# Polysketch attention, then a top-1 routed expert layer, on one core: a new hand-written order, fewer POOL rests behind the row scatters, and the zeroing of the row buffer in pieces

## The chip, the cores and the metric

The kernel runs on one core of a Trainium2 chip. The engines of the core run side by side, each through its own queue in order, and wait for one another on semaphores: TensorE (PE; its weight loads are listed as PEld), VectorE (DVE), ScalarE (ACT), GpSimd (POOL) and SyncE (SP, which here issues the loads). The metric is the device time of one execution in microseconds; lower is better. Before the change the median of five runs is 212.13 us (211.49 to 216.92).

## The reference

Four sequences of 1088 tokens with four heads of 32 numbers go through an attention without softmax. Each key and query is projected with two 8x32 matrices S1 and S2, and the outer product of the two projections (64 numbers, phi) takes its place. The result goes token by token through one of eight experts.

```
a = x @ S1.T;  b = x @ S2.T                        # x is q or k, per head
phi(x)[i*8 + j] = a[i] * b[j]
kv = sum over s of phi(k)[s] (x) v[s];   z = sum over s of phi(k)[s]
attn[s] = (phi(q)[s] @ kv) / (phi(q)[s] @ z + 1e-06)
x = attn as 4352 rows of 128 (four heads side by side)
logits = x @ w_gate;  e = argmax(logits);  gate = softmax(logits)[e]
out = gate * (relu(x @ w1[e]) @ w2[e])             # w1: 128x1024, w2: 1024x128, each of 8
```

## The kernel before

**Attention.** A batch b (0 to 3) is done in two chunks c of 512 tokens; the 64 tokens left of each batch go in pairs of batches r. Names in the order are made of these: k00 is the keys of batch 0, chunk 0; kr0 the left-over keys of batches 0 and 1; q and qr likewise. A chunk's steps (`features`, lines 347 to 399) are .t (PE turns four 128x128 blocks), .x (ACT copies them to SBUF), .a (PE projects, eight matmuls), .l (ACT copies the low part of the sums), .s (DVE adds it) and .o (DVE, L395, the outer product of 1024 numbers a partition). Keys then have .v (L404 and L408, PE: 40 small matmuls that add to kv), and a batch ends with e{b}: .r adds the left-over keys, .k copies (ACT), .t multiplies with the heads and the gate weights (PE), .c (ACT) and .m and .z (DVE) write the matrix kvx. Queries are turned in two halves (.T and .U on PE, .c and .d the copies on ACT), multiplied with kvx (.n and .N, PE, L522 or L526), and then divided: .p (ACT), .e (DVE reciprocal), .g (DVE, gate logits, L546) and .y (DVE, the 128 numbers of the row, L552), each with a 2 behind it for the second half.

**Routing.** r{b} finds the expert of each token of batch b: .a and .b (DVE: maximum and one-hot, L606), .x (ACT) and .c (DVE) the gate weight, .p (PE, L620 and L622) counts the tokens before each, .d (DVE, L635) makes the row number. Then r{b}.s{u} are eight or nine scatters on POOL (L641): each sends 128 rows of 130 words (128 numbers, gate weight, token number) to their place in the DRAM buffer xs_dram, where each expert has its own stretch of 4352 rows. The first 128 rows of each stretch are filled beforehand, with zeros and a token number that names no token, by one DMA on SP (L981) from the tile fill.

**Experts.** Tiles j of 128 rows are read back from xs_dram and go through one expert each. Tiles 0 to 9 need batches 0 and 1 in xs_dram, 10 to 17 batch 2 too, and from 18 on all four. A tile's steps (`expert_tile`, lines 816 to 922): .l (SP, L824, load of xg), .x (PE turns it, L846), .c (ACT copy), .w (DVE copies w1 of the expert, L858), .u and .U (PE, L863, two banks of eight matmuls), .r and .q (Relu; .q on DVE from tile 10 on), .d (PE, L898, sixteen matmuls with w2, into the bank py; its address in w2 is read from a table by each engine that needs it, L811), .y (ACT scales by the gate weight) and .s (POOL, L912, scatter to the output). 34 tiles always run. Up to seven more stand in three optional parts of 4, 2 and 1 tiles (`part`, line 1007), each under a branch (L1010). With this data the part of four is skipped and the other two run; it stands behind the .U of tile 25 and ahead of the .d of tile 24. t0, t1 and t2 (DVE) count which tile belongs to which expert.

**What sets the order.** The program is put out step by step as the list ORDER (line 20) has it; each engine's queue gets its part of that. After the last name of ORDER a loop (line 1037) puts out the rest. Buffers are taken from rings in the order of the program: a step that takes one of the eight PSUM banks waits for the step that last read it. Behind a scatter POOL does a number of small MEMSETs on one row of fill (`breathe`, line 563): three behind those of batches 0, 2 and 3, one behind those of batch 1 (`RESTS`), and two behind the output stores of tiles 0 to 11. On SP the first loads are put out at once, then the fill, then k, v and q of batch 3 as their buffers come free, then the left-over rows of batches 2 and 3 (k_rem, v_rem, q_rem), then the weights of the experts.

Of the kernel before, what the change touches and what calls it, by code (L numbers as in the profile page):

```python
# [17 lines left out]


ORDER = """  # L20
S.t k00.t k00.x S.m k01.t k01.x k00.a kr0.t k00.l kr0.x k00.s k00.o k01.a k01.l kr0.a k01.s k01.o q00.t q00.x
kr0.l q01.t k00.v q00.a k10.t q01.x q01.a k01.v kr0.s kr0.o q00.l q00.s e0.r k11.t k10.x q00.o q01.l q01.s
k10.a q01.o e0.k e0.t e0.m q00.U k11.x k11.a e0.z k10.l k10.s k10.o e0.c q00.d q01.U k11.l q01.T k11.s k11.o
q00.N q00.T q01.d q01.N q01.c q00.p2 q00.e2 q00.y2 q00.c q01.p2 q00.g2 q01.e2 q01.y2 q01.g2 q01.n q01.p q01.e
q01.g q01.y q00.n q00.p qr0.t q11.t q21.t qr0.x qr0.a q20.t q11.x q11.a q20.x q00.e q00.g r0.a r0.x r0.b r0.c
k31.t qr0.l qr0.s q00.y r0.p r0.d r0.s7 r0.s2 r0.s1 r0.s5 r0.s0 r0.s6 r0.s3 r0.s4 k10.v k11.v e1.r k31.x qr0.o
q21.x q21.a q11.l q11.s kr1.t qr0.T e1.k q10.t q21.l q20.a q10.x e1.t q11.o q21.s q20.l q21.o e1.c q11.U e1.m
e1.z q10.a qr0.c q11.d q11.T kr1.x q20.s q20.o q10.l q10.s k30.t q11.c k30.x qr0.n qr0.p k20.t q10.o qr0.e
qr0.y qr0.g q11.N kr1.a q11.p2 q11.e2 kr1.l kr1.s k20.x q11.y2 q11.n q11.p q10.U q10.d k30.a k30.l q11.g2
q10.T q11.e q10.c q11.y k30.s q20.T q10.N k30.o q10.p2 q10.e2 q11.g q10.g2 q10.y2 k21.t k21.x q10.n q10.p  # L30
k20.a q31.t q20.c q10.e q10.g r1.a r1.b q31.x k31.a q21.T r1.x k31.l kr1.o r1.c q30.t q30.x k31.s k21.a q10.y
# [9 lines left out]
j2.s j1.s t1.d j5.l j3.U j3.q j4.u j5.x j5.c j4.U j4.q j7.l j6.x j6.c j4.r r3.p q30.y j9.l j8.l r3.c j7.x j5.w
j5.u j7.c j5.r j5.U j5.q r3.d r3.s2 r3.s6 j3.d r3.s1 j6.w j6.u j4.d j6.r j3.y j7.w j6.U j11.l j0.y j0.s j8.x
j8.c j9.x j9.c j6.q j7.u j10.l j8.w j4.y r3.s4 j9.w j7.U j12.l j10.w j5.d t2.a t2.b t2.c t2.d j7.q j5.y j7.r
j8.u j8.U j11.w j11.x j9.u j9.U r3.s8 j12.w j5.s j9.q j6.d j6.y j13.l j10.x j10.c j12.x j12.c j7.d j8.q j10.u
j10.U j15.l j11.c j13.w r3.s5 r3.s3 j11.u j10.q j8.r j8.d j12.u j12.U j9.r j9.d j8.y j12.r j10.r j11.U j11.q
# [13 lines left out]


@with_exitstack
def kernel(
# [155 lines left out]
    for b in range(B):  # L218
        t = new(f"x_rows{b}", [128, J + 1, XW])
        x_rows.append(t)  # L220
        lgh.append(lgh[b - 2] if b > 1 else new(f"lgh{b}", [128, J + 1, H * E]))
# [125 lines left out]
    def features(x, n, srcs, take_dst, keeps):  # L347
        st = {}

        @op(x + ".t")  # L350
        def _():
            t = st["tp"] = banks.take()
            for i, s in enumerate(srcs()):
                nc.tensor.transpose(t[:, ts(i, 128)], in_=s, identity=ident)  # L354
# [35 lines left out]
        def _():  # L390
            s = st["s"]
# [3 lines left out]
            nc.vector.tensor_tensor(dst, a[:, :, :, None].broadcast_to([128, n * 4, R, R]),  # L395
                                    b[:, :, None, :].broadcast_to([128, n * 4, R, R]), ALU.mult)
# [419 lines left out]
    def expert_tile(j):  # L816
# [75 lines left out]
        @op(x + ".d")  # L892
        def _():
            r = word(tiles[j][0], [PE], (E - 1) * F)
            t = s["py"] = banks.take()
            for c in range(8):
                h = s["hTa"] if c < 4 else s["hTb"]
                nc.tensor.matmul(t[:, :DM], lhsT=h[:, ts(c % 4, 128)], rhs=w2_all[:, ds(r + c * DM, DM)],  # L898
# [181 lines left out]
```

## Time and profile before

| what | value |
|---|---|
| median of five runs | 212.13 us |
| the profiled execution | 211.94 us, of which the span from the first to the last instruction is 210.1 us |
| granted clock of TensorE in it | 0.999 |
| PE busy | 199.6 us (95%), 2107 matmuls |
| PEld busy | 195.2 us (93%) |
| DVE busy | 120.1 us (57%) |
| ACT busy | 80.2 us (38%) |
| POOL busy | 106.9 us (51%), 108 of its instructions the MEMSETs of 240 ns |
| DMA | 23.32 MB, 111 GB/s over the span |

The shares are means over stages that differ: until about 69 us attention and routing run, with many short steps that pass from engine to engine, and behind it the expert tiles. So a stage's table and the timeline tell more than the shares. A line of the timeline gives the start, the duration, the engine, the line of the kernel, the operation with its operands, a count of like instructions in a row, and in brackets the idle time of the engine before it with what ended that. "issue" is time in which the engine waited for nothing that the profile shows. A "q" behind an engine's name is its sequencer (branches, semaphores, register loads).

### The profile page before, as it was taken

What the parts mean: (1) busy time and instruction counts of PE and PEld (TensorE: products, weight loads), DVE (VectorE), ACT (ScalarE), POOL (GpSimd) and SP (SyncE); (2) the same over time, 40 slices, a digit from 0 to 9 for tenths busy, and PEclk for the clock granted to TensorE, in tenths of its full rate; (3) what the DMA queues carried; (4) which work ended last, traced back from release to release, by engine and by line L of the source; (5) the groups of instructions that cost most, each with busy time, mean ns of one, the idle gap of its engine ahead of it and who ended that gap; (6) DMA issues with size and microseconds to landing.
All of it is one profiled execution on the core that took longest, in us unless ns stands there. A gap on an engine that the chain in (4) does not pass through costs nothing. (4 is left out here: it accounts for less than half of the span.)

```text
span 210.1 us, 6120 instructions
## 1 busy us (share of the span) xinstructions
PE 199.6 (95%) x2107; PEld 195.2 (93%) x2107; DVE 120.1 (57%) x381; ACT 80.2 (38%) x218; POOL 106.9 (51%) x211
## 2 busy tenths in 40 slices
PE   7999979999798999999999999999998999999991
PEld 7799869998697999999999999999997999999991
DVE  4598896889988887998105324346245433251410
ACT  2456437563443635342332243332332333223220
POOL 6100047767940477868767776878521264046043
PEclk9999999999999999999999999999999999999999
DMA  4999989999712200021011102123310120001000
GB/s 148 295 317 276 257 225 268 370 377 382 272 45 75 63 28 25 30 76 51 28 51 43 39 29 75 50 66 102 95 46 16 36 60 15 0 16 36 17 24 16
DMA packets 29279, 23.32 MB, mean 111 GB/s; under 512 B 5866, under 2 KB 27116, under 8 KB 29248
## 3 DMA queue, kind: packets, MB, share of 16 engines
q1 hardware_dynamic: 26304, 18.15, 30.6%
q0 software_dynamic: 2400, 4.50, 6.4%
q8 instruction: 19, 0.31, 0.6%
q10 hardware_dynamic: 544, 0.26, 0.4%
q14 instruction: 12, 0.10, 0.2%
HBM read 17.81 MB, written 5.55 MB: 111 GB/s over the span
## 5 line engine op out<-in xcount | busy, mean ns | idle before, releaser
L863 PE MATMUL bank<-xgT,wide 128*128 128x128 f32 x592 | 72.3, 275 | 0.0
L863 PEld LDWEIGHTS bank<-xgT,wide 128*128 128x128 f32 x592 | 69.3, 192 | 0.0
L641 POOL DMA_INDIRECT xs_dram<-x_rows,row_i x34 | 35.9, 1056 | 46.1 <-DVE row_i L635 22.6
L889 DVE TENSOR_SCALAR hTb<-bank 128x512 f32<-128x512 f32 x27 | 18.6, 692 | 64.5 <-PE bank L863 44.6
L912 POOL DMA_INDIRECT out_dram<-y,to x23 | 22.7, 988 | 38.8 <-ACT xgT L851 20.2
L898 PE MATMUL bank<-w_all,hTa 128*128 x296 | 39.3, 276 | 0.9 <-DVEq L1010 0.9
L898 PE MATMUL bank<-w_all,hTb 128*128 x296 | 39.2, 275 | 0.0
L898 PEld LDWEIGHTS bank<-w_all,hTa 128*128 128x128 f32 x296 | 36.0, 192 | 1.2 <-issue 1.1
L898 PEld LDWEIGHTS bank<-w_all,hTb 128*128 128x128 f32 x296 | 36.0, 192 | 0.0
L907 ACT ACTIVATE y<-bank,xg 128x128 f32<-128x128 f32 x37 | 13.1, 368 | 54.4 <-PE bank L898 54.4
L880 ACT ACTIVATE hTa<-bank 128x512 f32<-128x512 f32 x37 | 21.9, 600 | 22.8 <-PE bank L863 19.7
L858 DVE COPY wide<-w_all 128x1024 f32 x39 | 27.6, 725 | 2.5 <-issue 2.3
L566 POOL MEMSET fill<- 1x130 f32 x108 | 26.0, 240 | 3.6
L912 POOL DMA_INDIRECT out_dram<-y,xg x18 | 18.5, 1029 | 9.3 <-issue 6.4
L395 DVE TENSOR_TENSOR wide<-sum 128x1024 f32<-128x1024 f32 (+1 forms) x18 | 20.4, 1139 | 0.6
L366 PE MATMUL bank<-s_cat,xT 128*128 128x128 f32 x136 | 19.0, 280 | 0.0
L366 PEld LDWEIGHTS bank<-s_cat,xT 128*128 128x128 f32 x136 | 16.7, 192 | 0.4 <-ACT xT L359 0.2
L522 PE MATMUL bank<-kvx,q_pT 128*128 128x82 f32 x128 | 15.4, 272 | 0.0
L522 PEld LDWEIGHTS bank<-kvx,q_pT 128*128 128x128 f32 x128 | 15.0, 192 | 0.0
L359 ACT COPY xT<-bank 128x512 f32<-128x512 f32 (+1 forms) x20 | 10.3, 526 | 9.6 <-PE bank L354 9.5
L851 ACT COPY xgT<-bank 128x128 f32<-128x128 f32 x41 | 10.0, 265 | 7.7 <-PE bank L846 7.5
L510 ACT COPY q_pT<-bank 128x512 f32<-128x512 f32 (+1 forms) x18 | 9.8, 567 | 1.5 <-PE bank L502 1.3
(156 smaller groups left out, 179.1 us busy)
## 6 DMA issues: line engine op xcount, KB each, us to landing
w_all<-in_moe_w_dram SPq DMA_DIRECT2D x16, 512.0 KB, 7.5
xg<-xs_dram SPq DMA_DIRECT2D x41, 65.0 KB, 1.8
wide<-in_v_dram SPq DMA_DIRECT2D x4, 512.0 KB, 5.6
wide<-in_q_dram SPq DMA_DIRECT2D x4, 512.0 KB
wide<-in_k_dram SPq DMA_DIRECT2D x3, 512.0 KB, 11.2
xs_dram<-fill SPq DMA_DIRECT2D x1, 585.0 KB
xs_dram<-x_rows,row_i POOLq DMA_INDIRECT x34
out_dram<-y,to POOLq DMA_INDIRECT x23
```

The lines of the kernel that those rows point to most:

```text
L366: nc.tensor.matmul(t[:, ts(i, 128)], lhsT=st["xT"][:, ts(i, 128)], rhs=s_cat.rearrange("p w t g r -> p (w t g r)"), start=True, stop=True)
L395: nc.vector.tensor_tensor(dst, a[:, :, :, None].broadcast_to([128, n * 4, R, R]), b[:, :, None, :].broadcast_to([128, n * 4, R, R]), ALU.mult)
L522: nc.tensor.matmul(o, lhsT=lhsT, rhs=kvx[b][:, hp].rearrange("p g c -> p (g c)"), start=True, stop=True)
L566: nc.gpsimd.memset(fill[0:1], 0.0)
L641: d = nc.gpsimd.indirect_dma_start(out=xs_dram[:], out_offset=bass.IndirectOffsetOnAxis(ap=st["row"][:, u:u + 1], axis=0), in_=x_rows[b][: ...
L858: nc.vector.tensor_copy(out=s["w1"], in_=w1_all[:, ds(r, F)])
L863: nc.tensor.matmul(t[:, ts(c, 128)], lhsT=s["w1"][:, ts(c0 + c, 128)], rhs=s["xT"], start=True, stop=True)
L880: nc.scalar.activation(s["hTa"], s["ha"], AF.Relu)
L889: nc.vector.tensor_scalar(s["hTb"], s["hb"], 0.0, None, ALU.max)
L898: nc.tensor.matmul(t[:, :DM], lhsT=h[:, ts(c % 4, 128)], rhs=w2_all[:, ds(r + c * DM, DM)], start=(c == 0), stop=(c == 7))
L907: nc.scalar.activation(s["y"], s["py"][:, :DM], AF.Copy, bias=0.0, scale=s["xg"][:, DM:DM + 1])
L912: d = nc.gpsimd.indirect_dma_start(out=out[:], out_offset=bass.IndirectOffsetOnAxis(ap=s["to"](), axis=0), in_=s["y"], in_offset=None, bou ...
```

## The change

- ORDER is another list of the same steps, carried a little further (up to j14.d as before, but with the first steps of tiles 16, 18 and 19 among them), with one drain of POOL in it.
- RESTS: no MEMSET behind the scatters of batch 0, two behind every other one of batch 1 (the second, fourth and so on), two behind those of batches 2 and 3.
- The bank py of tile 24 is taken ahead of the optional part of four tiles and not behind it.
- xs_dram is filled by two DMAs from x_rows3 (the rows of batch 3, zeroed by DVE at the start and given the token number that names none by POOL): eight rows of 520 bytes lie side by side in one run of 4160. They are put out behind the load of k of batch 3, no longer ahead of it. The true token numbers of x_rows3 are written by POOL after k11.o.
- The copies k00.x and k01.x are halved between DVE and ACT, and late_constants are put out after k01.x and no longer after S.m. S.m follows S.t at once.

```diff
 ORDER = """
...
-q01.g q01.y q00.n q00.p qr0.t q11.t q21.t qr0.x qr0.a q20.t q11.x q11.a q20.x q00.e q00.g r0.a r0.x r0.b r0.c
-k31.t qr0.l qr0.s q00.y r0.p r0.d r0.s7 r0.s2 r0.s1 r0.s5 r0.s0 r0.s6 r0.s3 r0.s4 k10.v k11.v e1.r k31.x qr0.o
-q21.x q21.a q11.l q11.s kr1.t qr0.T e1.k q10.t q21.l q20.a q10.x e1.t q11.o q21.s q20.l q21.o e1.c q11.U e1.m
...
-r1.p q21.c r1.d r1.s6 r1.s2 k20.l k20.s r1.s3 q31.a q20.U qr1.t r1.s8 qr1.x k21.l r1.s0 q20.d k30.v k20.o
-q30.a k20.v r1.s1 k21.s k21.o k21.v q31.l k31.o r1.s5 e2.r e2.k qr1.a q31.s q30.l e2.t q31.o e2.m e2.z t0.a
-q30.s q30.o k31.v t0.b t0.c e2.c e3.r q21.U e3.k e3.t e3.m q31.U q21.d q20.n q31.d qr1.l q21.n q21.p qr1.s
...
-qr1.T q31.p2 q31.e2 q31.g2 q31.y2 q30.p r2.x qr1.c q31.n q31.p q31.e q31.y r1.s7 q31.g q30.e2 q30.g2 r2.p j0.l
-j0.x j0.c r2.d j2.w r2.c r2.s5 qr1.n qr1.p j1.l j1.x j0.u j2.l j1.c j0.U j3.l j0.r r2.s2 t0.d j0.q j2.x j2.c
...
+q10.l q11.U q01.c q00.p2 q11.d q01.N q01.p2 q10.s q10.o q01.n q00.e2 q00.y2 q01.e2 q01.g2 q01.y2 qr0.t q00.g2
+q01.p qr0.x k10.v k11.v e1.r q01.e q01.g qr0.a e1.k qr0.l kr1.t kr1.x r0.a r0.b q10.U q10.d k20.t k20.x qr0.s
+qr0.o q10.T e1.t e1.m e1.z kr1.a e1.c r0.x q01.y q11.T r0.c r0.p r0.d r0.s1 r0.s7 r0.s6 r0.s2 r0.s0 r0.s3
...
+q21.l q21.s r1.x r1.c q30.x r1.d q31.a r1.s1 r1.s7 k21.l k21.s k21.o k31.x k20.v k31.a r1.s8 r1.s4 k30.x k30.a
+k21.v e2.r q31.l q31.s q31.o q20.x q20.a r1.s3 qr1.t q21.o k30.l k30.s q31.U e2.k e2.t k30.o e2.m qr1.x q21.U
...
+q30.l q30.s q20.U q31.c q20.d q21.n t0.a k30.v k31.v e3.r qr1.l q30.o q21.p qr1.s q20.T q20.N e3.k qr1.o e3.t
+e3.c q30.U q21.g2 q30.T e3.m e3.z qr1.T q21.e q31.d q20.c qr1.c q21.y2 t0.b q20.p2 t0.c q20.e2 j0.w q20.g2
+q30.c q31.n r1.s2 q31.p q31.e q21.y q20.y2 q31.g r1.s5 r1.s0 q21.g q20.n q20.p q20.e q31.N qr1.n j0.l q20.g
+q31.y q30.d q30.N q30.p2 q30.e2 q30.g2 q20.y q30.n q30.y2 j0.x j1.w r2.a r2.b j0.c t0.d j1.l j1.x j1.c j0.u
+j0.U j0.q j1.u j0.r j2.w j1.U q30.p q30.e r2.x r2.c j1.r q31.p2 r2.p r2.d r2.s4 r2.s2 qr1.p j4.w r2.s5 j2.l
...
-RESTS = (3, 1, 3, 3)
+RESTS = ((0,), (2, 0), (2,), (2,))
...
     zeros = new("zeros", [128, 128])
     nc.vector.memset(zeros, 0.0)
+    last_rows = new("x_rows3", [128, J + 1, XW])
+    nc.vector.memset(last_rows[:, 0:J], 0.0)
...
-    fill = new("fill", [128, XW])
-    nc.gpsimd.memset(fill, 0.0)
-    nc.gpsimd.iota(fill[:, DM + 1:DM + 2].bitcast(I32), pattern=[[0, 1]], base=ABSENT, channel_multiplier=0)
+    fill = new("fill", [1, XW])
+    nc.gpsimd.iota(last_rows[:, 0:J, DM + 1].bitcast(I32), pattern=[[0, J]], base=ABSENT, channel_multiplier=0)
...
-            nc.scalar.copy(out=st["xT"][:, :n * 128], in_=st["tp"][:, :n * 128])
+            half = 256 if x in ("k00", "k01") else 0
+            if half:
+                nc.vector.tensor_copy(out=st["xT"][:, :half], in_=st["tp"][:, :half])
+            nc.scalar.copy(out=st["xT"][:, half:n * 128], in_=st["tp"][:, half:n * 128])
...
-                breathe(RESTS[b])
+                breathe(RESTS[b][len(scattered[b]) % len(RESTS[b])])
...
-            t = s["py"] = banks.take()
+            if "py" not in s:
+                s["py"] = banks.take()
+            t = s["py"]
...
+    def fill_rows():
+        rows8 = last_rows[:, 0:J].rearrange("p j w -> p (j w)").bitcast(I32)
+        x4 = xs_dram.rearrange("(e n) w -> e n w", n=NTOK)
+        nc.sync.dma_start(out=x4[0:E, 0:128].rearrange("e (c j) w -> e c (j w)", j=J), in_=rows8)
+        nc.sync.dma_start(out=x4[E, 0:128].rearrange("(c j) w -> c (j w)", j=J), in_=rows8[0:128 // J])
...
                     load_main(nc.sync, n, src, b)
+                    if n == "k":
+                        fill_rows()
...
-        if name == "S.m":
+        if name == "k01.x":
             late_constants()
         if name == AFTER_LATE:
+            number_rows(B - 1)
             later_constants()
...
-    nc.sync.dma_start(out=xs_dram.rearrange("(e n) w -> n e w", n=NTOK)[0:128], in_=fill[:, None, :].bitcast(I32).broadcast_to([128, E + 1, XW]))
...
         for fn in ahead.pop(j, ()):
+            st[j]["py"] = banks.take()
             fn()
```

More of the change, by code (lines that the diff above doesn't have):

```diff
@@ L20 @@
 ORDER = """
[L21 to L24, printed above, removed]
-q01.g q01.y q00.n q00.p qr0.t q11.t q21.t qr0.x qr0.a q20.t q11.x q11.a q20.x q00.e q00.g r0.a r0.x r0.b r0.c
@@ L26 @@
-k31.t qr0.l qr0.s q00.y r0.p r0.d r0.s7 r0.s2 r0.s1 r0.s5 r0.s0 r0.s6 r0.s3 r0.s4 k10.v k11.v e1.r k31.x qr0.o
-q21.x q21.a q11.l q11.s kr1.t qr0.T e1.k q10.t q21.l q20.a q10.x e1.t q11.o q21.s q20.l q21.o e1.c q11.U e1.m
-e1.z q10.a qr0.c q11.d q11.T kr1.x q20.s q20.o q10.l q10.s k30.t q11.c k30.x qr0.n qr0.p k20.t q10.o qr0.e
-qr0.y qr0.g q11.N kr1.a q11.p2 q11.e2 kr1.l kr1.s k20.x q11.y2 q11.n q11.p q10.U q10.d k30.a k30.l q11.g2
-q10.T q11.e q10.c q11.y k30.s q20.T q10.N k30.o q10.p2 q10.e2 q11.g q10.g2 q10.y2 k21.t k21.x q10.n q10.p
@@ L31 @@
-k20.a q31.t q20.c q10.e q10.g r1.a r1.b q31.x k31.a q21.T r1.x k31.l kr1.o r1.c q30.t q30.x k31.s k21.a q10.y
-r1.p q21.c r1.d r1.s6 r1.s2 k20.l k20.s r1.s3 q31.a q20.U qr1.t r1.s8 qr1.x k21.l r1.s0 q20.d k30.v k20.o
-q30.a k20.v r1.s1 k21.s k21.o k21.v q31.l k31.o r1.s5 e2.r e2.k qr1.a q31.s q30.l e2.t q31.o e2.m e2.z t0.a
-q30.s q30.o k31.v t0.b t0.c e2.c e3.r q21.U e3.k e3.t e3.m q31.U q21.d q20.n q31.d qr1.l q21.n q21.p qr1.s
-e3.z q21.e q21.y q21.g q21.N j0.w q20.N q20.p2 qr1.o e3.c q20.p j1.w q20.e q20.y q30.U q30.d q20.g q21.p2
@@ L36 @@
-q21.e2 q30.T q30.c q31.T r1.s4 q31.N q21.g2 q20.e2 q31.c q30.N q30.p2 q20.g2 r2.a q30.n r2.b q21.y2 q20.y2
-qr1.T q31.p2 q31.e2 q31.g2 q31.y2 q30.p r2.x qr1.c q31.n q31.p q31.e q31.y r1.s7 q31.g q30.e2 q30.g2 r2.p j0.l
-j0.x j0.c r2.d j2.w r2.c r2.s5 qr1.n qr1.p j1.l j1.x j0.u j2.l j1.c j0.U j3.l j0.r r2.s2 t0.d j0.q j2.x j2.c
-j1.u qr1.e j3.x r2.s3 qr1.g q30.y2 j1.U j2.u j0.d r2.s6 q30.e j4.l j2.U j3.c r2.s4 j3.w j3.u j1.r j2.r r2.s7
-j1.q j2.q qr1.y j3.r j4.w j6.l j4.x j4.c t1.a t1.b r2.s0 q30.g r2.s1 r3.a r3.b r3.x t1.c j1.d j2.d j2.y j1.y
@@ L41 @@
[L41 to L45, printed above, removed]
@@ L46 @@
-j15.x j11.r j13.x j13.c j10.d j15.c j14.l j14.x j17.l j12.q j14.c j13.u j7.y j13.U j3.s j11.d j12.d j16.l
-j13.q j13.r j14.w j14.u j14.U j14.r r3.s0 r3.s7 j16.x j15.w j12.y j14.q j15.u j15.r j13.d j16.c j17.x j17.c
-j17.w j15.U j14.d
+S.t S.m k00.t k00.x k01.t k01.x k00.a kr0.t k01.a k00.l k00.s kr0.x kr0.a k00.o kr0.l kr0.s kr0.o q00.t q00.x
+k01.l k01.s k01.o q01.t k00.v q01.x q00.a q00.l q00.s k11.t q00.o k10.t k10.x q01.a q01.l q01.s k01.v k11.x
+e0.r q01.o e0.k k10.a k10.l k10.s k10.o q10.t q11.t q10.x q11.x e0.t e0.c e0.m e0.z k11.a k11.l q00.T q00.c
@@ new lines @@
+q11.a q01.U k11.s k11.o q00.U q00.n q11.l q11.s q10.a q11.o q01.T q00.d q00.N q00.p q00.e q00.y q00.g q01.d
+q10.l q11.U q01.c q00.p2 q11.d q01.N q01.p2 q10.s q10.o q01.n q00.e2 q00.y2 q01.e2 q01.g2 q01.y2 qr0.t q00.g2
+q01.p qr0.x k10.v k11.v e1.r q01.e q01.g qr0.a e1.k qr0.l kr1.t kr1.x r0.a r0.b q10.U q10.d k20.t k20.x qr0.s
+qr0.o q10.T e1.t e1.m e1.z kr1.a e1.c r0.x q01.y q11.T r0.c r0.p r0.d r0.s1 r0.s7 r0.s6 r0.s2 r0.s0 r0.s3
+kr1.l kr1.s kr1.o qr0.T r0.s5 q11.c qr0.c q11.N q11.p2 q10.c q11.n q11.p qr0.n q11.e2 q11.g2 q11.y2 q11.e
@@ new lines @@
+q11.y q11.g qr0.p qr0.e qr0.y qr0.g q21.t q21.x q10.n q10.p q10.e q10.N q10.p2 r0.s4 q31.t q31.x k20.a q10.g
+k20.l q10.y k21.t q30.t q10.e2 k30.t q10.y2 k21.x q21.a q20.t k21.a q10.g2 r1.a r1.b r1.p k20.s k20.o k31.t
+q21.l q21.s r1.x r1.c q30.x r1.d q31.a r1.s1 r1.s7 k21.l k21.s k21.o k31.x k20.v k31.a r1.s8 r1.s4 k30.x k30.a
+k21.v e2.r q31.l q31.s q31.o q20.x q20.a r1.s3 qr1.t q21.o k30.l k30.s q31.U e2.k e2.t k30.o e2.m qr1.x q21.U
+r1.s6 e2.z e2.c q20.l q20.s q21.d qr1.a q30.a q20.o q31.T k31.l k31.s q21.T q21.c q21.N k31.o q21.p2 q21.e2
@@ new lines @@
+j2.x qr1.e j2.c j3.l j5.l j1.q r2.s3 j0.d q31.e2 j0.y q31.g2 j2.u j2.r q31.y2 t1.a j2.U j3.w j4.l r2.s0 qr1.g
+j5.x j6.l j2.q j1.d j4.x j4.c j3.x j3.c j2.d j2.y j7.l j1.y j5.c j3.u j3.r j3.U t1.b t1.c j4.u j6.x j6.c q30.y
+j4.r j4.U qr1.y j8.l j7.x j7.c j5.w j5.u j5.r r2.s6 j5.U j6.w j9.l j3.q j6.u j6.U q30.g r3.a r3.x j8.x j8.w
+j3.d j0.s r2.s7 j9.x r2.s1 j8.c j6.q j2.s j4.q j5.q j7.w j7.u j7.r j4.d j4.y j5.d r3.b j10.l j4.s j3.y j3.s
+j5.y t1.d r3.p j9.w j8.u j7.U j6.r j6.d r3.c j9.c j9.u j7.q j1.s r3.d j10.w j8.U j8.r r3.s5 j6.y j11.w j9.U
@@ new lines @@
+j12.w r3.s3 r3.s0 r3.s1 r3.s2 j11.l r3.s7 j12.l j12.x j10.x t2.a j10.c r3.s6 j11.x j12.c j7.d j10.u j13.l
+j10.U j7.y j11.c j11.u j12.u j12.U j11.r j13.w j10.q j15.w r3.s8 j5.s j8.q j11.U j14.l j14.x j14.w j16.l j9.q
+j8.d j9.r j9.d j13.x j10.r r3.s4 j10.d j15.l j12.q j15.x j13.c j6.s drain j11.q j13.u j14.c j8.y j13.r j14.u
+j10.y j14.U t2.b j15.c j14.q j12.r j13.U j11.d j12.d j17.l j12.y j16.x j13.q j15.u t2.c j13.d j15.U j16.w
+j14.r j15.r j15.q j17.x j16.c j19.l j18.l j16.u j16.U j19.w j16.q j17.w j17.c j14.d t2.d
@@ L213, with number_rows @@
     iota(jio, [[1, NI]])
-    fill = new("fill", [128, XW])
-    nc.gpsimd.memset(fill, 0.0)
-    nc.gpsimd.iota(fill[:, DM + 1:DM + 2].bitcast(I32), pattern=[[0, 1]], base=ABSENT, channel_multiplier=0)
+    fill = new("fill", [1, XW])
+    nc.gpsimd.iota(last_rows[:, 0:J, DM + 1].bitcast(I32), pattern=[[0, J]], base=ABSENT, channel_multiplier=0)
     x_rows, lgh = [], []
[L218 to L221, printed above, removed]
+    def number_rows(b):
+        t = x_rows[b]
         nc.gpsimd.iota(t[:, 0:J, DM + 1].bitcast(I32), pattern=[[1, J]], base=b * S, channel_multiplier=J)
@@ L226 @@
                                base=(b - 1 + i) * S + MAIN, channel_multiplier=1)
+    for b in range(B):
+        t = last_rows if b == B - 1 else new(f"x_rows{b}", [128, J + 1, XW])
+        x_rows.append(t)
+        lgh.append(lgh[b - 2] if b > 1 else new(f"lgh{b}", [128, J + 1, H * E]))
+        if b < B - 1:
+            number_rows(b)
     def warm(n):
```

## The prediction

> **What bounds the kernel now.** I read the busy time by stretch first, then the timeline of TensorE (PE), then DVE, GpSimd (POOL) and the loads around each hole. By stretch (us, then PE, PEld, DVE, ACT, POOL busy, PE clock, DMA share, GB/s):
>
> ```profile
> 20.00:31.00 11.00, 9.32 (x165) 8.72 (x164) 9.76 (x42) 4.80 (x14) 1.90 (x5) 1.00 1.05 227
> 31.00:50.00 19.00, 19.00 (x222) 18.27 (x220) 15.26 (x45) 11.83 (x32) 13.60 (x31) 1.00 1.03 341
> 50.00:56.00 6.00, 4.64 (x168) 3.88 (x168) 5.68 (x15) 1.48 (x7) 5.29 (x10) 1.00 1.05 363
> 56.00:69.00 13.00, 12.36 (x128) 11.82 (x123) 11.43 (x46) 5.78 (x22) 4.21 (x6) 1.00 0.26 72
> 69.00:160.00 91.00, 91.00 (x825) 90.99 (x824) 49.22 (x169) 33.29 (x91) 60.26 (x115) 1.00 0.18 51
> 160.00:162.00 2.00, 1.05 (x9) 0.89 (x9) 0.85 (x2) 0.28 (x1) 0.00 (x0) 1.00 0.12 30
> ```
>
> PE sets the time. From 69 us on it has one hole, at 160; before, a few, and there DVE is nearly as full. The amount of PE work is untouched, so the change is worth the holes that it closes less those that it opens. These are the holes (start, duration, line, count, and in brackets the idle time before and who ended it):
>
> ```profile
> 7.93 0.30 PE L354 MATMUL bank<-ident,k_rem 128*128 128x128 f32 x1 [0.39 <-DMA k_rem<-in_k_dram]
> ...
> 25.66 0.63 PE L354 MATMUL bank<-ident,wide 128*128 128x128 f32 x4 [0.36 <-DVE sh L591]
> 26.45 0.19 PE L620 MATMUL bank<-oh,upper 128*128 128x64 bf16 x1 [0.17 <-DVE oh L606]
> ...
> 30.51 0.30 PE L354 MATMUL bank<-ident,k_rem 128*128 128x128 f32 x1 [1.15 <-DMA k_rem<-in_k_dram]
> ...
> 50.92 0.65 PE L404 MATMUL bank<-wide,wide 128*32 128x64 f32 x32 [0.19 <-DVE wide L395]
> ...
> 54.43 0.37 PE L404 MATMUL bank<-wide,wide 128*32 128x64 f32 x11 [1.17 <-issue]
> ...
> 65.78 0.19 PE L620 MATMUL bank<-oh,upper 128*128 128x64 bf16 x1 [0.37 <-DVE oh L606]
> ...
> 67.22 0.33 PE L846 MATMUL bank<-ident,xg 128*128 128x128 f32 x1 [0.17 <-DVE x_rows L552]
> ...
> 161.49 0.68 PE L898 MATMUL bank<-w_all,hTa 128*128 x4 [0.95 <-DVEq L1010]
> ```
>
> A dense matmul lasts 0.28 us, but the next starts 0.11 us after it (16 of L863 in 1.79), so a hole costs about 0.17 us more than its bracket. In order that is 0.56, 0.53, 0.34, 1.32, 0.36, 1.34, 0.54, 0.34 and 1.12, and 0.31 more at 66.54 (0.42 after the matmul at 66.12, less 0.11). All sums are made against the profiled execution: 210.1 us span and 1.84 around it, 211.94, which is 0.19 under the median of 212.13.
>
> **The start: 0.** k00 and k01 get half of their copy on DVE (128x512 takes ACT 0.53), so k00.a can start some 0.2 us earlier. But kr0.t behind it waits for k_rem until 7.93, and k00.s on DVE still stands behind the heads constant, which waits for w_gate until 8.44; neither load moves. The zeroing of x_rows3 on DVE (1040 numbers a partition; between 0.17, the row of 128, and 1.23, the row of 1024) falls into DVE's idle 0.34 and 0.93 us before 2.58. Without that cover up to 1.1 us would show.
>
> **The k remainder: about as now, +0.2.** PE reaches kr1.t today at 30.51 - 1.32 = 29.19. In the new order q10.t, q10.a and q11.U (1.79 us of PE) come ahead of it, and k31.t, q20.t, q21.t, q21.a, r0.p (2.54) no longer; the holes of 0.53 and 0.34 lie behind too. So PE arrives at 29.19 - 0.75 - 0.87 = 27.6. The load stands on SP's queue behind the fill, old and new. The old fill is 1152 rows of 520 B; while it ran (18.0 to 23.4) the DMA moved 201 GB/s, 336 just before. That is 1.09 MB, of which 0.6 MB is fill; the rest at 336 takes 1.45 us, so the fill took some 3.9. In runs of 4160 B, at the full 336 GB/s, it is 1.8. So k_rem lands between 28.3 (2.2 earlier) and 30.5 (nothing gained), and PE waits 0.7 to 2.9 us. I take 1.5, a little below the middle, since scatters, whose packets are also of 4160 B, run in the full stretch beside 341 GB/s.
>
> By the Trainium skill ("DMA: Bandwidth & Descriptors", section "Why a DMA increments its semaphore by 16 and not by 1") a DMA uses the largest number of engines up to 16 that divides both slowest dimensions. That speaks against these pieces: the first has 8 experts outermost against 128 partitions, so 8 engines, and by that an estimated 3.2 us in place of 1.8, k_rem at 29.7 and a wait of 2.1. No row of before shows it.
>
> **Group r0: -0.87.** r0.p now has 5.96 us of other PE work ahead (k10.v, k11.v, e1.r, e1.t, kr1.t, kr1.a, k20.t, q10.t, q10.a, q11.U, q10.U, q10.T, q11.T) and loses 1.37 (k31.t, q20.t, q21.t). DVE's one-hot gets only the s and o of q10 and q11 ahead: twice 1.6 us (28.37 to 29.97). So 4.6 against 3.2: a margin of 1.4 over a wait of 0.34. k31.t goes 15 us of PE work later.
>
> **k20.v to e3.r: -1.70, and +0.4 back.** Today four k.v groups stand between 50.0 and 55.1, and PE halts inside the last with no releaser but "issue" (1.34). Each is 40 small matmuls in 0.65 us. The new order puts 1.8 us of other PE work between the two of batch 2, and 6.8 us between those and the two of batch 3. Bounds of what remains: 0 (k10.v, k11.v and e1.r ran back to back from 26.76 without it) and 1.34; I take 0.4, nearer to the first, as at most two now follow each other. The 0.36 before k21.v also goes.
>
> **Group r2 and the first tiles: -1.19.** r2.p gets u and U of j0 and j1 (four times 0.89), their two transposes (0.22) and qr1.n (0.43) ahead: 4.23 us. DVE's one-hot gets q20.y2, q21.y2, q30.y2, q31.y (0.34 each), q31.e, q30.e2 (0.24), q31.g, q30.g2 (0.15): 2.1 us. So 2.1 us of margin stands against the wait of 0.54. The banks of j0.x, qr1.n and j1.x were those of y2 copies issued just before; those now come earlier.
>
> **What comes late next: +0.6.** With PE ahead, DVE is next: it is busy 15.3 of 19 and 11.4 of 13 us. Adding up such durations along both engines in the new order leaves DVE 0.3 to 1.7 us ahead at the other handovers. One of the tightest: e3.m and e3.z (0.17 and 0.34, and two handovers of some 0.1) can start when e3.t has ended, and PE has q30.U, q30.T and qr1.T (1.1 us) until q31.n needs them: 0.4. Bounds: 0, and 3.8, the sum of the DVE and issue holes of today. I take 0.6: two handovers missed by 0.3.
>
> **The bank ahead of the optional part: -0.1 of 1.12.** With four tiles skipped, tile 24 gets a bank last read by DVE in a skipped tile; now it gets that of tile 22. But PE itself has three steps at the branch (L1010, L811): it waits for its own matmuls until 160.6, bumps semaphores until 160.8, and loads w2's address from 160.9 for 0.302; that load is not moved. DVE's bump comes at 161.3, the matmul at 161.46. Bounds 0 and 1.12; the rows put the own path at 161.3 or later.
>
> **Rests and scatters: 0.** 42 of 108 MEMSETs of 0.24 us go, on an engine that is never the last. A scatter with its rests takes 2.24 us with three (33.75 to 35.98), 2.06 with two (90.55 to 92.61), 1.33 with one (49.30 to 50.64), 1.28 with none (147.49 to 148.77). r0.p comes at 26.45 + 4.6 - 0.87 + 1.5 = 31.7, and the first scatter about 1 us later, at 32.7. Eight at 1.28 and eight gaps of batch 1 (four of each kind) put the last at 56.3, landing at 58.5 (today 59.52, and j0.l follows at 61.82). PE reaches j0.x at 66.12 - 3.1 + 1.2 = 64.2 and needs j0.l by 62: 3.5 us of slack. Behind it 23 scatters and stores at 2.06 from 69.2 end by 118; j18.l is needed near 124 (j18.x today 128.5). The added drain and the indices that move to POOL's long idle stretch (21.83 us before 28.42) cost nothing. The t2 steps go to DVE's half-empty stretch after 69; without that cover they cost what they take of DVE, at most the 10.7 us from 87.2 to 97.9 in which they run now.
>
> **Sum.** -0.87 - 1.70 - 1.19 - 0.1 + 0.2 + 0.4 + 0.6 = -2.7, so 209.2.
>
> **Rivals.**
> *All waits go*, the load's too: 0.87 + 1.70 + 1.19 + 1.32 + 0.1 = 5.2, 206.8. For it: every margin above is positive. Against: PE only comes sooner to loads whose path is hardly shorter. Chance 0.14.
> *The order trades waits*: DVE is the true bound until 69 us and misses its handovers by what the old order lost, 3.1 us in place of 0.6: 211.7 (211 to 213). For it: DVE is busy 9.76 of 11 us and 5.68 of 6. Chance 0.19.
> *Slower: the scatters keep their pace without rests, or worsen.* j0.l needs all 17. If descriptors, not rests, set their period, 17 at 2.06 from 32.7 put the last at 65.7, landing at 67.9, and j0.x waits 5.9 us: 209.2 + 5.9 = 215. It decides from a mean period of about 1.7 us on (slack used up) and makes it slower than before from about 1.85 (3.5 + 2.7 over 16 gaps, above 1.48). Against: 1.33 and 1.28 in the rows. Chance 0.12.
> *Forecast* 0.55, 207.9 to 210.6.
>
> The range runs from 206.6 to 213.0; that leaves out the slower rival and the edges. About 0.5% (1.06 us) is what a measurement of this kernel can tell from no change. Faster: 0.54 of the forecast, 0.14, and 0.02 of the traders, 0.70. Same: 0.12 of the traders and 0.01, 0.13. Slower: 0.05 of the traders and 0.12, 0.17.
>
> **What would show it.** The k_rem hole below 0.7 or above 2.9 us; holes at L620, L846 and the issue hole gone or not; the hole at 160 still near 1; scatters of batch 0 at 1.28 apart; any hole of over 1 us at an L846 after 64 us would make the prediction wrong through the scatters, several of 0.3 to 1 us on DVE through the order.

## The result, and the profile after

The changed kernel takes 211.57 us (median of 52 runs, 209.44 to 213.44), the kernel before beside it 212.23 (94 runs). The ratio is 0.9963, with a 95% interval of 0.9947 to 0.9978: 0.8 us less, clear of no change by the interval, but not 2.9 us, and less than the 1.06 us that the prediction named as what can be told from no change. The ratio leaves out the runs that fell in a slower state, 34 of the 94 (214.1 to 217.8 us) and four of the changed kernel's (213.0 to 213.4). The profiled execution took 210.17 us, span 208.4, against 211.94 and 210.1: there the gain is 1.8.

That difference has a reason. Each run lists the clock that was granted to TensorE, and the changed kernel's runs fall into two groups: of 54 listed with their clock 20 took 209.4 to 210.7 us at 0.996 to 0.998, 30 took 211.0 to 212.4 us at 0.988 to 0.992 (four more took 213 us at 0.984). Such groups are not new with the change: in a later list the kernel before takes 212.2 to 212.6 us at 0.995 to 1.000 and 213.2 to 214.0 at 0.987 to 0.991. The profiled execution is of the first group. So there are two questions: where 0.9 us of the forecast's gain went in that execution, and what costs another 1.6 us in six runs of ten.

The busy times by stretch, columns as in the prediction:

```profile
20.00:31.00 11.00, 10.88 (x181) 10.31 (x180) 9.95 (x38) 6.08 (x18) 0.34 (x3) 1.00 0.82 249
31.00:50.00 19.00, 19.00 (x270) 18.26 (x268) 17.05 (x52) 10.26 (x30) 13.61 (x13) 1.00 1.06 362
50.00:56.00 6.00, 6.00 (x133) 5.74 (x130) 5.72 (x15) 3.03 (x10) 4.59 (x8) 1.00 0.75 255
56.00:69.00 13.00, 11.23 (x105) 10.36 (x105) 10.62 (x46) 5.37 (x18) 3.29 (x5) 1.00 0.20 53
```

PE has become full where it had its holes: 10.88 of 11 us in place of 9.32, and 6.00 of 6 in place of 4.64. But between 56 and 69 us it lost: 11.23 in place of 12.36. The timeline of PE shows where (start, duration, line, operation, count, idle time before and who ended it):

```profile
8.19 0.30 PE L360 MATMUL bank<-ident,k_rem 128*128 128x128 f32 x1 [0.69 <-DMA k_rem<-in_k_dram]
...
28.20 0.30 PE L360 MATMUL bank<-ident,k_rem 128*128 128x128 f32 x1
...
64.63 0.30 PE L855 MATMUL bank<-ident,xg 128*128 128x128 f32 x1 [1.29 <-DMA xg<-xs_dram]
65.33 0.30 PE L855 MATMUL bank<-ident,xg 128*128 128x128 f32 x1 [0.40 <-DMA xg<-xs_dram]
...
159.70 1.15 PE L909 MATMUL bank<-w_all,hTa 128*128 x8 [0.84 <-PEq L820]
```

The lines of the changed kernel lie some 9 further down: L360 is the old L354, L650 the scatter L641, L833 the load L824, L855 the .x of a tile (L846), L404 the outer product (L395). The holes at the rank counts and among the k.v groups are gone, and k_rem's second wait (1.15) no longer shows. New are 1.29 and 0.40 us in front of the first two tiles, 2.0 us with the 0.17 that each hole costs beyond its bracket. They wait for xg, which SP may load only when all 17 scatters of batches 0 and 1 have landed:

```profile
33.00 1.33 POOL L650 DMA_INDIRECT xs_dram<-x_rows,row_i  x1 [7.38 <-DVE sum L391]
...
38.46 0.97 POOL L650 DMA_INDIRECT xs_dram<-x_rows,row_i  x1 [0.30 <-issue]
39.73 2.00 POOL L650 DMA_INDIRECT xs_dram<-x_rows,row_i  x1 [0.30 <-issue]
42.04 0.97 POOL L650 DMA_INDIRECT xs_dram<-x_rows,row_i  x1 [0.30 <-issue]
43.32 1.80 POOL L650 DMA_INDIRECT xs_dram<-x_rows,row_i  x1 [0.30 <-issue]
...
50.31 1.88 POOL L650 DMA_INDIRECT xs_dram<-x_rows,row_i  x1 [0.30 <-issue]
...
59.65 0.97 POOL L650 DMA_INDIRECT xs_dram<-x_rows,row_i  x1 [0.55 <-issue]
```

The first scatter starts at 33.00 (forecast 32.7), the last at 59.65 (forecast 56.3). The periods of 1.28 and 2.0 us are there, but five of the 17 scatters last 1.29 to 2.00 us and not 0.97: 0.36 + 1.03 + 0.83 + 0.32 + 0.91 = 3.45 us more. SP issues the first xg at 62.59, after 1.8 us of waiting for the scatters' rows; PE is ready from 63.34 on, and its matmul on xg starts 2.0 us behind the issue:

```profile
62.59 8.43 SPq L833 DMA_DIRECT2D xg<-xs_dram  x10
```

DVE's timeline at these moments:

```profile
39.67 1.23 DVE L404 TENSOR_TENSOR wide<-sum 128x1024 f32<-128x1024 f32 x1
...
43.05 1.23 DVE L404 TENSOR_TENSOR wide<-sum 128x1024 f32<-128x1024 f32 x1
...
50.12 1.23 DVE L404 TENSOR_TENSOR wide<-sum 128x1024 f32<-128x1024 f32 x1
```

The scatter of 39.73 starts just behind the outer product of 39.67, which runs on until 40.90, 1.17 us later; the scatter is 1.03 longer. At 43.32, 0.96 us of a product are left, and the scatter is 0.83 longer; at 50.31, 1.04 and 0.91. Each time it is the rest of the product less 0.13, and so it is at 45.42 (0.45 left, 0.32 longer). The scatter of 33.00 starts with 0.29 us left of a shorter product (256 numbers), which accounts for 0.16 of its 0.36; it is also the first after 7.38 us of idle time, and in the kernel of its own below the first of all, beside nothing, lasts 1.13. Scatters that start beside other work of DVE last 0.97.

### The profile page after: what moved, and what is told of

Read it like the earlier page. It is cut to its first block, busy times and chain, and to the rows that moved or that the text cites. A ratio compares the mean times of both kernels' runs of the same rounds, so it can differ in the third digit from the quotient of the medians.

```text
span 208.4 us, 6077 instructions
## 1 busy us (share of the span) xinstructions
PE 199.6 (96%) x2107; PEld 195.4 (94%) x2107; DVE 121.5 (58%) x384; ACT 79.4 (38%) x218; POOL 97.3 (47%) x168
## 5 line engine op out<-in xcount | busy, mean ns | idle before, releaser
L872 PE MATMUL bank<-xgT,wide 128*128 128x128 f32 x592 | 71.3, 275 | 0.0
L650 POOL DMA_INDIRECT xs_dram<-x_rows,row_i x34 | 36.9, 1087 | 31.7 <-issue 14.4
L404 DVE TENSOR_TENSOR wide<-sum 128x1024 f32<-128x1024 f32 (+1 forms) x18 | 20.3, 1135 | 0.5
L575 POOL MEMSET fill<- 1x130 f32 x66 | 15.3, 232 | 1.9
L531 PE MATMUL bank<-kvx,q_pT 128*128 128x82 f32 x128 | 15.9, 274 | 0.1
L368 ACT COPY xT<-bank 128x512 f32<-128x512 f32 (+2 forms) x20 | 9.9, 502 | 8.1 <-PE bank L360 3.4
L855 PE MATMUL bank<-ident,xg 128*128 128x128 f32 x41 | 9.8, 275 | 1.7 <-DMA xg<-xs_dram 1.7
```

The costliest lines, as they stand in the source:

```text
L531: nc.tensor.matmul(o, lhsT=lhsT, rhs=kvx[b][:, hp].rearrange("p g c -> p (g c)"), start=True, stop=True)
L575: nc.gpsimd.memset(fill[0:1], 0.0)
L650: d = nc.gpsimd.indirect_dma_start(out=xs_dram[:], out_offset=bass.IndirectOffsetOnAxis(ap=st["row"][:, u:u + 1], axis=0), in_=x_rows[b][: ...
L872: nc.tensor.matmul(t[:, ts(c, 128)], lhsT=s["w1"][:, ts(c0 + c, 128)], rhs=s["xT"], start=True, stop=True)
```

## Experiments

**Theory.** The scatters have become what ends last ahead of j0.x. Their pace is set by POOL's rests and by DVE's products, which hold them. The clock falls behind the hole that this leaves in PE. **Rivals:** the DMA's backlog, not the pace of the scatters, sets the landing; the wait for k_rem went because of the new order and not of the fill; the lower clock has another place.

### Batch 1's scatters without rests

```diff
-RESTS = ((0,), (2, 0), (2,), (2,))
+RESTS = ((0,), (0,), (2,), (2,))
```

> Batch 1's scatters without rests, once more, since in the first runs both kernels stood at 229 to 236 us with holes that nothing released. Theory: last scatter at 56.7 in place of 59.65, the holes at j0.x and j1.x (1.45 and 0.59) go, 2 us less than the changed kernel: 208.2 where the clock is 0.996 or more. Rival (backlog of the DMA): hole over 1 us, time as the changed kernel's. Whether the group of times at the lower clock also goes tells whether the hole at 64 us brings the slow spell.

Measured: 208.87 us (five runs, 208.81 to 209.04), ratio to the kernel before 0.9809 (0.9774 to 0.9844). The last scatter, SP's load and PE's first tile, in this order:

```profile
57.00 0.97 POOL L650 DMA_INDIRECT xs_dram<-x_rows,row_i  x1 [0.30 <-issue]
```

```profile
60.74 8.43 SPq L833 DMA_DIRECT2D xg<-xs_dram  x10
```

```profile
63.41 0.55 PE L855 MATMUL bank<-ident,xg 128*128 128x128 f32 x2 [0.17 <-DMA xg<-xs_dram]
```

The last scatter starts 2.65 us earlier, and of 1.69 us of waiting 0.17 is left. Closer scatters do land sooner; the rival of the backlog falls. xg itself is issued only 1.85 us earlier, since SP does not wait for the scatters any more: DVE writes the row number of the first tile at 59.58 to 59.75, and SP, which has to read it, issues xg 1.0 us later. Another run, with the changed kernel beside it:

> Batch 1's scatters without rests, beside the changed kernel on the same chip. Theory: 208.9 us, within 0.3 us in all executions, at a clock of 0.996 or more in all of them: without the hole at 64 us there is no second group of times. Rival: a second group, some 1.6 us later, stays.

Measured: 208.94 us (four runs, 208.79 to 209.07), ratio 0.9867 (0.9844 to 0.9890). All nine runs of the two lists lie within 0.3 us, at a clock of 0.996 to 1.000. With the hole the second group of times is gone too, as it is in the four runs of "The first tiles' rows sooner" below (0.995 to 0.999), where the wait is 0.56 us.

### The clock behind the hole

> The changed kernel unchanged, for a profile of an execution at a granted clock of 0.988 to 0.992, where no engine waits for instructions. Theory: a hole of 1.4 and 0.6 us at j0.x and j1.x and behind it 3 to 4 us at a clock of 0.5 in six executions of ten, 211.8 us; in the others the same holes and no such spell, 210.1. Rival: the clock is 0.5 elsewhere, behind k_rem's hole at 8 or at the optional part.

Measured: 210.51 us (11 runs, 209.76 to 212.87), ratio 0.9956 (0.9917 to 0.9995); six runs took 209.76 to 210.51 at 0.996 to 0.998, five 211.36 to 212.87 at 0.984 to 0.992. The profiled execution is one of these (211.40 us, 0.990). PE's first two tiles in it, and then the busy times by stretch (PE is the first pair, the granted clock the third number from the end):

```profile
64.11 0.30 PE L855 MATMUL bank<-ident,xg 128*128 128x128 f32 x1 [1.20 <-DMA xg<-xs_dram]
64.94 0.30 PE L855 MATMUL bank<-ident,xg 128*128 128x128 f32 x1 [0.53 <-DMA xg<-xs_dram]
```

```profile
64.00:65.00 1.00, 0.35 (x2) 0.22 (x3) 0.98 (x2) 0.27 (x1) 0.00 (x0) 1.00 0.33 85
65.00:66.00 1.00, 1.00 (x7) 1.00 (x8) 0.88 (x4) 0.27 (x1) 0.00 (x0) 0.70 0.40 102
66.00:67.00 1.00, 1.00 (x7) 1.00 (x6) 0.83 (x8) 0.00 (x0) 0.00 (x0) 0.50 0.30 79
67.00:68.00 1.00, 1.00 (x7) 1.00 (x7) 0.69 (x2) 0.00 (x0) 0.00 (x0) 0.50 0.30 75
68.00:69.00 1.00, 1.00 (x7) 1.00 (x7) 0.16 (x1) 0.56 (x2) 0.00 (x0) 0.60 0.21 47
```

The holes are as long as in the first profile. Behind them the clock stands at half for some 3.4 us, and PE does 7 matmuls a microsecond: 0.30 + 0.50 + 0.50 + 0.40 = 1.7 us of work lost, which is the distance between the two groups. In the first profile the same stretch has a clock of 1.00:

```profile
66.00:67.00 1.00, 1.00 (x11) 1.00 (x10) 0.89 (x5) 0.00 (x0) 0.00 (x0) 1.00 0.28 70
```

Only this one execution of the slower group was profiled; for the others only the mean clock speaks, whose 0.008 less over 209 us is the same 1.7 us. No other spell at half clock lies in this execution before PE's last matmul.

### The old rests in the changed kernel

```diff
-RESTS = ((0,), (2, 0), (2,), (2,))
+RESTS = ((3,), (1,), (3,), (3,))
```

> The rests of before in the changed kernel, once more. Theory: last scatter at 62 to 64 us, xg at 66 to 68.5, PE waits 3 to 5 us at j0.x: 212 to 214 us. Rival (rests off the path): within 0.5 us of the changed kernel.

Measured: 220.49 us (four runs, 219.69 to 222.12), ratio 1.0378 (1.0313 to 1.0444). The sign and the mechanism held, the size did not. The last scatter starts at 64.66, xg is issued at 67.22, and PE waits:

```profile
69.24 0.45 PE L855 MATMUL bank<-ident,xg 128*128 128x128 f32 x1 [5.77 <-DMA xg<-xs_dram]
...
135.51 0.30 PE L855 MATMUL bank<-ident,xg 128*128 128x128 f32 x1 [2.49 <-DMA xg<-xs_dram]
```

Seven of the 17 scatters were held by DVE (1.48 to 1.69 us each in five of them), which I had put at two or three. The clock was 0.50 from 66 to 72 us, and the rests of batches 2 and 3 open a second hole, at 135. In this order the rests, which the forecast priced at nothing, are worth 9 us, with what the clock loses behind the holes.

### The new rests in the kernel before

> Kernel before with the rests of the changed kernel alone, once more. Theory and forecast: nothing hangs on the scatters there: holes unchanged, time within 0.4 us of before. Rival: closer scatters crowd the loads of 31 to 56 us and PE's holes grow by over 0.5 us.

Measured: 213.01, 216.09, 216.44 and 217.27 us at clocks of 0.996, 0.983, 0.984 and 0.967; the kernel before takes 211.34 to 212.30 in its nine runs at 0.994 or more. So at a full clock one run alone says slower, by 0.7 us over the slowest of those; the trace of the run of 216.09 shows why, against the theory and the forecast alike. POOL, then SP:

```profile
38.69 0.98 POOL L641 DMA_INDIRECT xs_dram<-x_rows,row_i  x1 [0.30 <-issue]
48.21 0.98 POOL L641 DMA_INDIRECT xs_dram<-x_rows,row_i  x1 [8.54 <-DVE row_i L635]
...
62.77 0.97 POOL L641 DMA_INDIRECT xs_dram<-x_rows,row_i  x1 [0.17 <-issue]
```

```profile
66.28 8.42 SPq L824 DMA_DIRECT2D xg<-xs_dram  x10
```

PE at this tile, and the clock there:

```profile
68.17 0.45 PE L846 MATMUL bank<-ident,xg 128*128 128x128 f32 x1 [1.78 <-DVE lgh L546]
```

```profile
68.00:69.00 1.00, 0.83 (x7) 0.64 (x9) 0.93 (x7) 0.27 (x1) 0.00 (x0) 0.50 0.30 69
```

Batch 0 is done sooner, but batch 1 can't begin before its row numbers, at 48 us in either kernel, so POOL stands idle for 8.54 us. From there one rest costs next to nothing (a period of 1.33), while two behind every other scatter cost half of 0.7 each time, some 2.4 us in all. With 0.25 us at the start and 0.6 us of longer scatters the last one starts 3.25 us later than before (62.77 against 59.52), xg is issued at 66.28 and not 61.82, and PE waits 1.78 us at j0.x. The profile puts that wait to DVE's lgh at 67.95; but in the kernel before the same matmul runs at 66.12, ahead of the same lgh at 67.72, so it is xg, which lands 1.7 us behind its issue. Behind this wait and one of 1.18 us at 66.02 (for DVE's one-hot) the clock is 0.50 from 67 to 74 us. This part of the change, alone, costs time.

### The fill, each way

The new fill alone in the kernel before:

> Kernel before with the new fill alone, once more. Theory: SP issues k_rem 2.9 us earlier, the hole at kr1.t (1.31) falls below 0.4, the others stay: 0.9 to 1.1 us less than before. Rival: the hole stays over 0.9, time within 0.3 us.

Measured: 211.57 us (12 runs, 210.31 to 215.58), ratio 0.9916 (0.9881 to 0.9950), that is 1.8 us (1.1 to 2.5): more than the 0.9 to 1.1 expected, which only touches the lower end of the interval. The hole at kr1.t is gone: the transpose of k_rem at 28.67 us has no wait. (Behind that this profile is no guide to the time, since its clock is 0.50 from 53 to 67 us.) The whole change gains 0.8 us (ratio 0.9963), so the fill alone, in the kernel before and in another session, gains at least as much as everything together. The rival, that the order took this wait away, falls. The old fill in the changed kernel (zeroed, placed and put out as before):

> Changed kernel with the old fill (rows of 520 bytes, issued ahead of batch 3's k). Theory: k_rem comes at 30.5 as before, PE is at kr1.t by 28.2, so a hole of 2.2 us in place of 0.28; but what PE loses there it doesn't wait for at j0.x, since the scatters hang on r0.p, which moves too by what the hole costs: so part of the loss stays: 1 to 2 us slower than the changed kernel. Rival: the new order alone had taken the wait away, the hole stays under 0.6 and the time within 0.3 us.

Measured: 215.19 us (four runs, 214.57 to 216.30), ratio 1.0121 (1.0064 to 1.0179), which is 3.4 us more than the changed kernel's ratio gives, where 1 to 2 us were expected. PE's line, and the stretch behind it:

```profile
30.83 0.44 PE L358 MATMUL bank<-ident,k_rem 128*128 128x128 f32 x1 [2.40 <-DMA k_rem<-in_k_dram]
```

```profile
31.00:34.00 3.00, 3.00 (x17) 2.67 (x18) 0.00 (x0) 1.44 (x3) 0.00 (x0) 0.50 0.73 235
```

The wait of 2.40 is as expected (2.2), but behind it the clock is 0.50 for three microseconds. The first scatter moves from 33.00 to 37.27: 4.3 us for a wait of 2.4.

### What holds a scatter

A kernel of its own: six scatters of 128 rows in a row, while one engine does one thing back to back.

```
for work in (nothing, products, copies, psum_products, psum_evictions, reductions, act_copies):
    start work; for _ in range(6): scatter 128 rows of 520 bytes
```

> No reference output (only 128 rows of zeros are stored): seven groups of six scatters of 128 rows of 520 bytes each, without rests, while DVE or ACT does one thing back to back: nothing; the product of two inputs in SBUF (128x1024); copies SBUF to SBUF (128x1024); products of one input in PSUM and one in SBUF (128x512); evictions of PSUM alone (128x512); sums over one input in SBUF; copies on ACT. Theory: a scatter that starts while DVE reads two inputs from SBUF is held until that operation ends, so 0.97 us with nothing, with ACT and with PSUM alone, and 1.0 to 2.1 us each beside the products (1.23 us); the copies of 128x1024 (0.69 us) hold too, up to 0.6 us. Rival: the longer scatters in the changed kernel came from the DMA's load, not from DVE; then all seven groups are alike within 0.1 us.

The first scatters beside the products and the copies, two each, and then the first beside each of the four other kinds of work; the products began at 9.46 and 10.71 (1.22 us each), the copies at 22.40 (0.68):

```profile
9.55 1.98 POOL L70 DMA_INDIRECT xs_dram<-x,row  x1 [0.19 <-issue]
11.83 0.98 POOL L70 DMA_INDIRECT xs_dram<-x,row  x1 [0.30 <-issue]
...
22.80 1.13 POOL L70 DMA_INDIRECT xs_dram<-x,row  x1 [0.51 <-issue]
24.24 1.15 POOL L70 DMA_INDIRECT xs_dram<-x,row  x1 [0.30 <-issue]
...
36.36 0.99 POOL L70 DMA_INDIRECT xs_dram<-x,row  x1 [0.55 <-issue]
...
50.20 0.99 POOL L70 DMA_INDIRECT xs_dram<-x,row  x1 [0.55 <-issue]
...
63.66 0.98 POOL L70 DMA_INDIRECT xs_dram<-x,row  x1 [0.55 <-issue]
...
76.61 0.98 POOL L70 DMA_INDIRECT xs_dram<-x,row  x1 [0.54 <-issue]
```

At 9.55 a product has 1.13 us to go, and the scatter lasts 1.00 longer, until 11.53. So the next one starts at 11.83, 0.1 us ahead of the end of the second product, and is free, and so are the rest: the period of 1.28 keeps in step with the products' 1.26. I had expected each of the six to be held; that was wrong. All six beside the copies in SBUF (0.69 us each) last 1.13 to 1.16, 0.16 to 0.19 longer. Beside products with one input in PSUM (from 36.36), evictions of PSUM (50.20), sums over one input (63.66) and copies on ACT (76.61) every scatter lasts 0.97 to 0.99. So not DVE being busy holds a scatter, nor the DMA's load, but two kinds of operation: products of two inputs in SBUF, and copies within SBUF.

### The first tiles' rows sooner

```diff
-e3.c q30.U q21.g2 q30.T e3.m e3.z qr1.T q21.e q31.d q20.c qr1.c q21.y2 t0.b q20.p2 t0.c q20.e2 j0.w q20.g2
+e3.c q30.U q21.g2 q30.T e3.m e3.z t0.b t0.c qr1.T q21.e q31.d q20.c qr1.c q21.y2 q20.p2 q20.e2 j0.w q20.g2
```

(and batch 1 without rests)

> Batch 1 without rests and t0.b, t0.c earlier, once more. Theory: the holes left at j0.x (0.33 and 0.30) close; 0.2 to 0.5 us less than batch 1 without rests alone (208.87). Rival: the DVE steps put off make PE wait: same or up to 0.5 us more.

Measured: 208.85 us (four runs, 208.66 to 209.02), ratio 0.9858 (0.9835 to 0.9881): the same as without the move. xg is issued at 60.39 in place of 60.74, as the row number is there 0.36 us sooner, but now j0.x waits 0.56 us for DVE's x_rows (L561). The rival was right: what comes sooner on DVE puts off something else.

### Runs that settle nothing

In two sessions all kernels, the one before among them, took 221 to 236 us, with holes of up to 4 us around 40 us and, in most, more at 150, which the profile puts to "issue"; the other sessions' profiles show no "issue" hole over 1.2 us. So no verdict is drawn from these times. The first session:

> The changed kernel once more, for a second profile of it. Its single times fall into two groups: about 210.1 us with a granted clock of 0.996 to 0.998, and about 211.8 us with 0.988 to 0.992. The first profile is of the first group (210.17, 0.996). If this one is of the second group, the theory expects one spell of 3 to 5 us at a clock of 0.5 just behind the hole at 62 to 66 us, in which PE's dense matmuls take twice as long, and otherwise the same holes. Rivals: the slow spell lies at the start or at the optional part (then the hole at 64 us has no part in it), or there is none and one of the holes is longer by 1.6 us.

> Changed kernel, batch 1's scatters without rests. Theory: the wait of j0.x and j1.x (holes of 1.45 and 0.59 us) stands because the last of the 17 scatters starts at 59.65 us, 3.3 later than forecast. Four rests pairs of 0.73 us fewer put it at 56.7; it lands by 59.3, xg by 61.5, PE arrives at 63.3. So both holes go, 2.0 us less in the profiled execution (208.2 against 210.17), and the median falls by 2 at least (209.6 or less against 211.57). Rival, the DMA's backlog sets the landing: scatters closer together land no sooner, the hole stays over 1 us and the time stays within 0.5 us of the changed kernel's.

> Changed kernel with the rests of before (three behind each scatter of batch 0, one behind those of batch 1, three later). Theory: the scatters end last in front of j0.x, so their pace counts. Eight periods of 2.24 and eight of 1.33 from 33.0 us put the last at 61.6 without any scatter held by DVE, with two or three such at 63 to 64; xg then lands at 66 to 68.5, and PE, there at 63.3, waits 3 to 5 us in place of 1.45: 212 to 214 us. Rival, rests off the critical path (as the forecast had it, 3.5 us of slack): within 0.5 us of the changed kernel.

> Kernel before with the new fill of the rows alone (pieces of 4160 bytes from the zeroed x_rows3, issued behind batch 3's k). Theory: the old fill of 520-byte rows held the load of k_rem; the hole at kr1.t (1.31 us at 30.5) falls below 0.4 and the other holes stay, so the time falls by 0.9 to 1.1 us (211.2). Rival: the hole at kr1.t went in the changed kernel because of the new order, not of the fill; then the hole stays over 0.9 and the time within 0.3 us.

Measured there: 222.76 us for the changed kernel, and ratios to the kernel before (232.59) of 0.9994 (0.9943 to 1.0045) for batch 1 without rests, 0.9940 (0.9886 to 0.9995) for the old rests and 0.9867 (0.9776 to 0.9959) for the new fill. The second:

> The changed kernel unchanged, for a profile of an execution of its second group (about 211.8 us, granted clock 0.988 to 0.992; some 6 in 10). Theory: behind the hole at 63 to 66 us PE's clock stands at 0.5 for 3 to 4 us, which costs 1.5 to 2 us; where the profile is of the first group (210.2 us) there is no such spell, and the same holes. Rival: the clock is 0.5 elsewhere.

> Kernel before with the rests of the changed kernel alone. Theory and forecast agree: there PE reaches j0.x at 66.1 us and j0.l is issued at 61.82, so nothing hangs on the scatters: holes unchanged, time within 0.4 us of before. Rival: closer scatters crowd the loads of 31 to 56 us (k_rem or the later inputs come later) and PE's holes grow by over 0.5 us.

> Batch 1's scatters without rests, and in the order the steps t0.b and t0.c moved from behind q21.y2 to behind e3.z, so that the first tiles' rows are known some 0.9 us earlier (59.85 us without this). Theory: j0.l, issued at 60.74 behind the last scatter's landing and 0.4 behind its row, gains at most 0.4 us, and the holes left at j0.x (0.33 and 0.30) close: 0.2 to 0.5 us less than without the move (208.87). Rival: the DVE steps put off (q21.e, q21.y2, j0.w) make PE wait: same or up to 0.5 us more.

Measured: 222.05 us, 231.21 and 231.75 us beside 231.49; the changed kernel's ratio there is 0.9647 (0.9614 to 0.9680), that of batch 1 without rests and with t0.b, t0.c earlier 1.0018 (0.9968 to 1.0068). So in these sessions the changed kernel leads by 8 to 10 us, and batch 1 without rests is no better than the kernel before, unlike in the other sessions. Why these holes come, and why they cost the changed kernel less, stays open; what is said here of batch 1's rests holds for executions without them. One reading fits the rest: in the changed kernel's profile there PE waits at j0.x at 69 us, and the clock is 0.57, 0.50, 0.50 and 0.73 in the four microseconds from 70 on.

## Why the prediction was right or wrong

**The step that failed is "Rests and scatters: 0"**, with its 3.5 us of slack; in its place the runs show two holes in PE that cost 2.0 us, and, in six runs of ten, another 1.7 us of clock behind them. Three things ate the slack. The last scatter started 3.35 us later than put (59.65 against 56.3): 0.3 of this is the start, and 3.1 are scatters held by DVE's products, which I had not looked for. The rows that would have told it stood in the profile of before, among scatters of 0.97; I left them out of the period (DVE, then POOL):

```profile
30.42 1.23 DVE L395 TENSOR_TENSOR wide<-sum 128x1024 f32<-128x1024 f32 x1
```

```profile
30.85 1.64 POOL L641 DMA_INDIRECT xs_dram<-x_rows,row_i  x1 [0.57 <-issue]
...
56.13 1.69 POOL L641 DMA_INDIRECT xs_dram<-x_rows,row_i  x1 [0.17 <-issue]
```

Here too each lasts longer by the rest of a product less 0.13: 0.67 of 0.80, and 0.72 of 0.85 with a product that starts at 55.75. Then the load followed 2.9 us behind the last scatter's start, not 2.3 as before (59.52 to 61.82). And PE came 0.9 us earlier than put (63.34 against 64.2), since k_rem did not hold it. The rival that I called slower had the right place and the wrong mechanism: the mean period was 26.65 / 16 = 1.67 us, close to the 1.7 from which it was to decide, but through DVE and not through descriptors. The test that I named, a hole of over 1 us at an L846 after 64 us, is the one that struck.

**What that hole costs beyond itself** stood in no term: half clock for some 3.4 us in part of the runs, 1.7 us (shown by one profile, inferred for the others from their mean clock). The forecast's sum was made for one execution; the median is one of those with the slow spell.

**The k remainder, +0.2**, was wrong in sign: 1.32 went to under 0.3. The fill takes less of the DMA than the 1.5 us of waiting supposed: SP issues k_rem at 17.72 and not 20.61, it has landed by 28.2, the early end of my range, and between 18.0 and 23.4 us the DMA moves 363 GB/s where it was 201 (before, then after):

```profile
18.00:23.40 5.40, 5.40 (x52) 5.40 (x51) 4.72 (x20) 2.98 (x10) 0.00 (x0) 1.00 1.23 201
```

```profile
18.00:23.40 5.40, 5.40 (x51) 5.40 (x51) 4.93 (x19) 3.35 (x9) 0.00 (x0) 1.00 1.07 363
```

The estimate of 29.7 that the prediction worked out by a rule of the Trainium skill ("DMA: Bandwidth & Descriptors", "Why a DMA increments its semaphore by 16 and not by 1") did not come; on how many engines the fill ran no view shows. The fill alone is worth 1.8 us (1.1 to 2.5) in the kernel before, and in the changed kernel its undoing costs 2.4 us of waiting and three microseconds at half clock.

**Group r0 (-0.87), the k.v groups (-1.70), r2 and the first tiles' DVE waits (-1.19)**: all these holes are gone, as put; of the 0.4 and 0.6 us that were to come back no hole over 0.3 us on DVE is seen. But the holes that went and came add up to some 2.6 us (the 6.8 of the prediction's list less 0.86, 0.3, 1.46, 0.57 and 1.01), while the span fell by 1.7: the rest is spread over gaps of under 0.2 us between matmuls, and I have not traced it to a cause. **The bank, -0.1**: the hole at the branch went from 0.95 to 0.84, and PE's own path (PEq, L820) ends it now, as put. **The start, 0**: k_rem's first wait went from 0.39 to 0.69; it varies between the profiles of the changed kernel.

With the failed step mended (batch 1 without rests) the kernel takes 208.9 us, close to the forecast of 209.2; part of this agreement is luck, since the 1.2 us too much for k_rem and the 1.0 us that did not come back stand against the small gaps and the waits that remain.
